# Moving the table of gates by token behind the large SBUF pools

## The chip, the cores and the metric

The kernel runs on one core of one Trainium2 chip. The metric is the device time of one execution in microseconds (us); the time of a kernel is the median of its runs. Below, a profile of one execution is used beside it.

## The reference

Attention with a sliding window of 128 keys and 4 sink keys, for 4 batches, 8 heads, 768 tokens and a head width of 64; its output, 3072 tokens by 512, goes through a mixture of 4 experts, all of which are computed for each token and added with weights from a given table:

```python
keep = is_sink | in_window              # rel = query - key in [0, 128), or key < 4
scores = np.where(keep, scale * q @ k.T, -1e9)
a = softmax(scores);  x = a @ v         # x as [B*S, H*D] = [3072, 512]
p = domain_probs / (domain_probs.sum(-1, keepdims=True) + 1e-09)
for e in range(4):                      # w1[e] is 512 x 1024, w2[e] is 1024 x 512
    out += p[:, e:e + 1] * (np.maximum(x @ w1[e], 0.0) @ w2[e])
```

## The kernel before

Everything works on tiles of 128 partitions in bf16, with sums in PSUM in float32. Batches go one after another, each in three groups of 256 tokens, and for each group each of the four experts is a unit of work.

**Stages.** Queries, keys and values of a batch are loaded by POOL's queue with a cast from float32 to bf16 (`qkn`, line 267, and `vx`, line 331); the weights `w1` and `w2` likewise (lines 344 and 354). The first 256 tokens of q and k come in float32 by SP's and ACT's queues (line 292, tiles `qraw` and `kraw`) and are cast on DVE and ACT. Batch 0 is turned on TensorE (line 616); the later batches are turned by DMA transposes on SP's queue: `qkT` from `qkn` (line 276), `xT` from `onat` (line 806). Scores (line 719) go through ACT's exponential (line 747) into `aT`; `aT` is multiplied with the values `vx` (line 789) and, for the sink keys, `sinkA` with `vsd` (line 782).

**Experts.** The first product of an expert is made directly for early units (line 1134), later with seven products of half blocks (line 1224); for late units with the operands exchanged (line 1336), so that the result lies token by token. There it is multiplied by the gate of each token, one number for each partition, from `own_gates` (lines 1357 and 1361), and a DMA transpose turns it into `H` (line 1317). The other units multiply by rows of gates that were spread over all partitions (`gates`, lines 491, 1158 and 1257). The second product is line 1597 for the first two groups and line 1511 for the others.

**Order.** The kernel is planned in Python while it is written out: it keeps an estimated clock for each engine and for both kinds of DMA queue, and at each step emits the piece of work that is ready first, by fixed priorities. The order on every engine is thus fixed when the program is built. While TensorE would be idle in the first 20 us, idle products on a tile of zeros (`lent`, line 595) are put in.

**Where tiles lie in SBUF.** The pools are laid end to end, each tile rounded up to 32 bytes in every partition, in this order: `consts`, `wpool` (weights and their combinations), `attn_sb`, `moe_sb`, `odd`. The first free byte is 16512. In `consts` come first six tiles `vx` of 1056 bytes each (8 heads, 66 bf16 numbers for each head, of which 65 are used), then `own_gates` (18 x 4 float32, 288 bytes, line 327), then `gates0`, `gates1` (2048 bytes each), `ident`, `masks`, `ksd`. From the end of `own_gates` on, up to the pool `odd`, every tile has a size that is a multiple of 256 bytes.

Before, `own_gates` begins at byte 22848 and `gates0` at 23136, which is 96 past a multiple of 256, and so does each tile of the pools `wpool`, `attn_sb` and `moe_sb` after it. In the pool `odd` lie small tiles: `held`, `vsf` (the values of the sinks), `scale_t`, `sel2`, `half`, `own_sum`, six `R`, `vsd` and `rs`.

Small tiles that the change names: `scale_t` (line 511) holds the gates of the first two groups, loaded by SP at line 1691, made ready in `gates()` with `rs` (line 961) and read at lines 1607 and 1610. `sel2` (line 520) and `half` (line 579) are constants for the sinks; `held` (line 498) is the target of two small copies on POOL (line 1726), which make it wait.

Of the kernel before, what the change touches and what calls it, by code (L numbers as in the profile page):

```python
# [11 lines left out]
FP32 = mybir.dt.float32  # L12
BF16 = mybir.dt.bfloat16
# [3 lines left out]
def kernel(  # L17
# [17 lines left out]
    E, Dm, F = moe_w1.shape  # L35
    Ntok, Dout = out.shape

    P = 128
# [7 lines left out]
    NHP = H // 2  # L46
# [52 lines left out]
    NEARLY = 2  # L99
# [39 lines left out]
    def dve(cols, *deps, rate=0.96, fixed=157):  # L139
        at = max([t["dve"], *deps])  # L140
        t["dve"] = at + fixed - 77 + cols / rate
        return at + fixed + 60 + cols / rate

    def pool(cols, *deps, fixed=190):
        at = max([t["pool"], *deps])
        t["pool"] = at + fixed + cols * 1.8
        return t["pool"] + 35
# [96 lines left out]
    consts = ctx.enter_context(tc.tile_pool(name="consts", bufs=1))  # L244
# [3 lines left out]
    odd = ctx.enter_context(tc.tile_pool(name="odd", bufs=1))  # L248
# [75 lines left out]

    vx = [consts.tile([P, H, DP], BF16, name=f"vx{tb}") for tb in range(NQB)]
    OWNED = 2 * NG * (B - OWN)
    own_gates = consts.tile([P, OWNED, E], FP32, name="own_gates")

    def load_v(b, ts):
        for tb in ts:  # L330
            nc.gpsimd.dma_start(  # L331
                out=vx[tb][:, :, 0:D],
                in_=v[b, :, tb * P:(tb + 1) * P, :].rearrange("h p d -> p h d"),
            )
            lands(("v", b, tb), H * P, D, values_at[b - 1, min(NG - 1, (tb + 1) // 2)] if b else 0.0)
# [159 lines left out]
        gate_at[pair, e] = sp(mix.finished[mix.gated[len(gate_sb) - 1 - NGATE]] if len(gate_sb) > NGATE else 0.0, takes=300) + GATE_LANDS  # L495


    held = odd.tile([P, 2], BF16, name="held")
    nc.vector.memset(identf, 1.0)
    lent = wpool.tile([P, 12 * P], BF16, name="lent", tag=f"wf_{E - 2}")  # L500
    zeros = lent[:, 0:4 * P]
# [4 lines left out]
    for h in range(H):  # L506
# [1 line left out]
        nc.sync.dma_start(  # L508
            out=vsf[r:r + NSINK, :, 0:D], in_=v[:, h, 0:NSINK, :].rearrange("b j d -> j b d"),
        )  # L510
    scale_t = odd.tile([P, 2 * NEARLY, E], FP32, name="scale_t")
    ident = consts.tile([P, P], BF16, name="ident")
    load_v(0, (0,))
    for sgn in (1, -1):
# [2 lines left out]
            base=0, pattern=[[sgn, P]], channel_multiplier=-sgn,  # L517
        )
        pool(0, fixed=320)
    sel2 = odd.tile([P, NHP, 2], FP32, name="sel2")  # L520
    load_v(0, (1,))
    t["sw"] += 500
    for tb in (2, 3):
# [52 lines left out]
    t["dve"] += 240.0  # L576

    vsd = {}
    half = odd.tile([P, 2], BF16, name="half")
    ksd = [consts.tile([P, NHP, 32], BF16, name=f"ksd{i}") for i in range(2)]  # L580

    nc.vector.memset(half, 0.0)
# [375 lines left out]


    def gates():  # L960
        rs = odd.tile([P, 2 * NEARLY], FP32, name="rs")
        nc.vector.reduce_sum(out=rs, in_=scale_t, axis=AX.X)
        nc.vector.tensor_scalar_add(out=rs, in0=rs, scalar1=1e-9)
        nc.vector.reciprocal(out=rs, in_=rs)
        nc.vector.tensor_mul(scale_t, scale_t, rs[:, :, None].to_broadcast([P, 2 * NEARLY, E]))
        dve(200)
# [8 lines left out]
    class Mixture:  # L975
# [608 lines left out]
        def emit_second(self):  # L1584
            ready = self.second_ready()
            g, s, e = self.second.pop(0)
            if g not in out_sb:
                out_sb[g] = mo.tile([P, 2, Dout], FP32, name="osbw", tag=f"wide{g}", bufs=1)
                if g == 0:
                    gates()  # L1590
# [232 lines left out]
```

## Time and profile before

| | |
|---|---|
| median of 3 runs | 353.85 us (353.6 to 354.17) |
| profiled execution, device time | 354.31 us |
| its span, first to last instruction | 352.6 us |
| TensorE matmuls (PE) busy | 345.2 us, 98% |
| weight loads (PEld), DVE, ACT, POOL busy | 76%, 80%, 59%, 20% |
| DMA packets | 161800, of them 145508 under 512 bytes; 45.62 MB |
| granted TensorE clock | 1.000 |

The profile is that of one execution. "Busy" is the time from the start of an engine's instructions to their end; matmuls overlap one another, so a matmul's own duration (273 ns for 256 columns) is longer than the time from one to the next. The chain of waits follows the work back from the last instruction, at each step to what released it. A window names the busy time of each engine in a stretch of the span.

### The profile page before, as it was taken

How to read it: one execution, taken by the hardware profiler on the slowest of the kernel's cores; microseconds unless marked ns; L12 is line 12 of the kernel's file. 1: busy time of each engine (PE TensorE's matmuls, PEld its weight loads, DVE VectorE, ACT ScalarE, POOL GpSimd, SP SyncE). 2: the span in 40 equal slices, each digit the busy share in tenths (PEclk: the TensorE clock that was granted, in tenths of full speed). 3: DMA queues.
4: the chain of work that ended last, by engine and by line, in shares of the span. 5: the costliest groups of instructions: out<-in, count | busy, mean ns of one | idle time of the engine just before them, and what ended most of it. 6: DMA issues, size and time to landing. Idle time of an engine off the chain costs nothing.

```text
span 352.6 us, 9328 instructions
## 1 busy us (share of the span) xinstructions
PE 345.2 (98%) x3699; PEld 266.7 (76%) x3722; DVE 282.9 (80%) x672; ACT 207.5 (59%) x481; POOL 72.0 (20%) x89
## 2 busy tenths in 40 slices
PE   8999999999999999999999999999999999999996
PEld 4685869756798998899999886756856666666785
DVE  5785889988999999899799899488769594785740
ACT  4864813446645734856544559489589666757411
POOL 8946104340242351400144000000000000000000
PEclk9999999999999999999999999999999999999999
DMA  9999999999995999950799905339338838455431
GB/s 171 172 191 192 220 217 173 182 159 145 181 133 55 170 175 146 134 100 26 80 175 149 138 32 98 84 71 156 75 91 168 131 60 164 78 105 135 89 92 61
DMA packets 161800, 45.62 MB, mean 129 GB/s; under 512 B 145508, under 2 KB 157764, under 8 KB 161756
## 3 DMA queue, kind: packets, MB, share of 16 engines
q0 software_dynamic: 79104, 17.31, 55.2%
q1 hardware_dynamic: 81596, 27.19, 42.1%
q8 instruction: 29, 0.48, 0.6%
q10 hardware_dynamic: 1056, 0.52, 0.6%
q14 instruction: 15, 0.12, 0.1%
HBM read 38.40 MB, written 6.34 MB: 127 GB/s over the span
## 4 chain that ended last, share of the span: by engine, by line
PE 89%; DMA 3%; POOL 2%; ACT 2%; DVE 1%; issue 1%; POOLq 0%; ACTq 0%
PE acc L1511 34%; PE cps L1224 18%; PE cps L1336 14%; PE hps L1134 8%; PE acc L1597 8%; PE sps L719 3%; PE od L789 3%; DMA w<-in_moe_w_dram 2%; POOL qkn L267 1%; POOL vx L331 1%; PE od L782 1%; DMA H<-rest 1%; DVE cps L1384 1%; PE sinks L680 0%; DVE gates L1361 0%
## 5 line engine op out<-in xcount | busy, mean ns | idle before, releaser
L1511 PEld LDWEIGHTS <-H 128*128 128x128 bf16 x708 | 66.2, 98 | 18.4 <-issue 1.6
L1511 PE MATMUL acc<-w,H 128*128 128x256 bf16 x420 | 57.3, 273 | 0.3 <-ACT acc L1550 0.2
L747 ACT ACTIVATE aT<-sps 128x512 bf16<-128x512 f32 (+1 forms) x96 | 47.4, 577 | 12.5 <-PE sps L719 12.4
L1224 PEld LDWEIGHTS <-w 128*128 128x128 bf16 x640 | 39.3, 98 | 1.7 <-issue 0.6
L1511 PEld LDWEIGHTS <-S 128*128 128x128 bf16 x320 | 30.8, 98 | 8.5
L1257 DVE SCALAR_TENSOR_TENSOR H<-cps,gates 128x512 bf16<-128x512 f32 x54 | 36.3, 684 | 0.6 <-PE cps L1224 0.4
L834 ACT ACTIVATE onat<-od,R 128x64 bf16<-128x64 f32 x120 | 27.4, 332 | 14.4 <-DVE R L816 11.9
L1134 PE MATMUL hps<-xT,w 128*128 128x256 bf16 x256 | 32.2, 273 | 0.7 <-DMA w<-in_moe_w_dram 0.7
L331 POOL DMA_DIRECT2D vx<-in_v_dram x24 | 21.3, 892 | 55.6 <-PE od L789 43.3
L1354 ACT ACTIVATE cps<-cps 128x512 f32<-128x512 f32 x41 | 23.8, 585 | 14.9 <-PE cps L1336 14.0
L1511 PE MATMUL acc<-wf,H 128*128 128x256 bf16 (+1 forms) x224 | 30.9, 271 | 0.1
L1224 PEld LDWEIGHTS <-vf 128*128 128x128 bf16 x480 | 29.2, 98 | 0.9 <-issue 0.5
L1597 PE MATMUL acc<-w,H 128*128 128x512 bf16 x121 | 29.2, 379 | 0.4
L1134 PEld LDWEIGHTS <-w 128*128 128x128 bf16 x256 | 24.0, 98 | 5.3 <-DMA w<-in_moe_w_dram 0.9
L739 DVE TENSOR_TENSOR aT<-aT,masks 128x1024 bf16<-128x1024 bf16 (+1 forms) x36 | 22.8, 644 | 4.4 <-ACT aT L747 4.2
L1572 ACT COPY osb<-acc 128x256 f32<-128x256 f32 x32 | 12.1, 379 | 22.8 <-PE acc L1511 22.7
L1224 PE MATMUL cps<-T,w 128*128 128x128 bf16 x320 | 24.3, 219 | 0.0
L1224 PE MATMUL cps<-T,vf 128*128 128x128 bf16 x320 | 23.8, 219 | 0.0
L1224 PE MATMUL cps<-xT,w 128*128 128x128 bf16 x320 | 23.7, 219 | 0.0
L267 POOL DMA_DIRECT2D qkn<-in_q_dram x22 | 19.7, 896 | 16.3 <-DMA qkT<-qkn 8.5
L1336 PE MATMUL cps<-w,T 128*128 128x512 bf16 x75 | 22.7, 379 | 0.1
L1336 PE MATMUL cps<-vf,T 128*128 128x512 bf16 x77 | 22.6, 379 | 0.1
(144 smaller groups left out, 673.1 us busy)
## 6 DMA issues: line engine op xcount, KB each, us to landing
w<-in_moe_w_dram POOLq DMA_DIRECT2D x6, 1024.0 KB, 18.6
out_dram<-osb SPq DMA_DIRECT2D x16, 256.0 KB
vx<-in_v_dram POOLq DMA_DIRECT2D x24, 128.0 KB, 6.6
qkn<-in_q_dram POOLq DMA_DIRECT2D x22, 128.0 KB, 6.9
qkn<-in_k_dram POOLq DMA_DIRECT2D x22, 128.0 KB, 7.2
gates<-gate_rows SPq DMA_DIRECT2D x20, 128.0 KB
w<-in_moe_w_dram POOLq DMA_DIRECT2D x4, 256.0 KB, 8.0
w<-in_moe_w_dram POOLq DMA_DIRECT2D x2, 512.0 KB, 11.4
```

Source lines behind the costliest of these rows:

```text
L267: nc.gpsimd.dma_start(out=nat[b, tb][:, i], in_=(q, k)[i][b, :, tb * P:(tb + 1) * P, :].rearrange("h p d -> p h d"),)
L331: nc.gpsimd.dma_start(out=vx[tb][:, :, 0:D], in_=v[b, :, tb * P:(tb + 1) * P, :].rearrange("h p d -> p h d"),)
L739: nc.vector.tensor_mul(x, x, m[:, None, :].to_broadcast([P, 2 if g == 0 else 4, w if g == 0 else 2 * P]))
L747: nc.scalar.activation(out=a[:, ph], in_=sps[ph][:, 0:w], func=AF.Exp, scale=scale)
L834: nc.scalar.mul(o[:, qi, hp, ph * D:(ph + 1) * D], od[:, qi, ph, 0:D], R[:, qi, ph])
L1134: nc.tensor.matmul(h[:, i].rearrange("p (q n) -> p q n", q=2), lhsT=w1_sb[e][:, db, fb * P:(fb + 1) * P], rhs=xT[b, g][:, :, db], start=(i ...
L1224: nc.tensor.matmul(y[:, f], lhsT=A[:, d, f * P:(f + 1) * P], rhs=T[:, d], start=(m in ("P1", "P5") and f == 0 and d == 0), stop=(d == 1), ...
L1257: nc.vector.scalar_tensor_tensor(out=dst, in0=src, scalar=0.0, in1=gate, op0=ALU.max, op1=ALU.mult)
L1336: nc.tensor.matmul(y.rearrange("p f n -> p (f n)"), lhsT=T[:, d], rhs=A[:, d], start=(m in ("P1", "P5") and d == 0), stop=(d == 1), skip_g ...
L1354: nc.scalar.activation(out=src, in_=src, func=AF.Relu)
L1511: nc.tensor.matmul(y, lhsT=self.operand(b, g, e, m)[:, f], rhs=forms[e][m][:, f, cs], start=(k == 0 and f == 0 and m in (("P1", "P5", "P2" ...
L1597: nc.tensor.matmul(op, lhsT=H[:, fb // QF, fb % QF, s], rhs=w2_sb[e][:, fb, :], start=(fb == 0), stop=(fb == NFB - 1),)
```

## The change

`own_gates` leaves the pool `consts` and becomes a tile of `odd`, the last pool. In its place stand five small tiles that were in `odd`. No instruction is added or taken away.

```diff
-    own_gates = consts.tile([P, OWNED, E], FP32, name="own_gates")
+    own_gates = odd.tile([P, OWNED, E], FP32, name="own_gates")
+    scale_t = consts.tile([P, 2 * NEARLY, E], FP32, name="scale_t")
+    sel2 = consts.tile([P, NHP, 2], FP32, name="sel2")
+    held = consts.tile([P, 2], BF16, name="held")
+    half = consts.tile([P, 2], BF16, name="half")
+    rs = consts.tile([P, 2 * NEARLY], FP32, name="rs")
...
-    held = odd.tile([P, 2], BF16, name="held")
...
-    scale_t = odd.tile([P, 2 * NEARLY, E], FP32, name="scale_t")
...
-    sel2 = odd.tile([P, NHP, 2], FP32, name="sel2")
...
-    half = odd.tile([P, 2], BF16, name="half")
...
 def gates():
-        rs = odd.tile([P, 2 * NEARLY], FP32, name="rs")
```

With each tile rounded up to 32 bytes the five take 64 + 32 + 32 + 32 + 32 = 192 bytes where `own_gates` took 288. So `gates0` begins at 23040 = 90 x 256, and all tiles behind it, up to the pool `odd`, lie 96 bytes lower than before. `vx` stays where it was. In `odd`, `own_gates` now begins at a multiple of 256, `vsf` goes from 128 to 32 past such a multiple, and `vsd` from 64 to 96 past it.

## The prediction

> **What bounds the kernel now.** I read the page first, for the engine that the time hangs on and for the chain of waits that ended last.
>
> ```profile
> span 352.6 us, 9328 instructions
> PE 345.2 (98%) x3699; PEld 266.7 (76%) x3722; DVE 282.9 (80%) x672; ACT 207.5 (59%) x481; POOL 72.0 (20%) x89
> ...
> PE 89%; DMA 3%; POOL 2%; ACT 2%; DVE 1%; issue 1%; POOLq 0%; ACTq 0%
> ```
>
> TensorE (PE) is busy for 98% of the span and has 89% of the chain. A change can help in two ways only: matmuls follow each other at shorter intervals, or PE waits less. So I next took the windows, to see how much waiting there is and where.
>
> ```profile
> 0.00:18.25 18.25, 15.59 (x151) 9.09 (x152) 12.12 (x55) 11.95 (x28) 16.58 (x24) 1.00 1.68 173
> 18.25:40.00 21.75, 21.59 (x228) 15.50 (x230) 15.50 (x47) 14.04 (x28) 10.08 (x13) 1.00 1.56 197
> 40.00:90.00 50.00, 49.67 (x499) 36.02 (x504) 45.39 (x90) 22.62 (x54) 13.15 (x15) 1.00 1.63 178
> 90.00:210.00 120.00, 119.95 (x1736) 108.87 (x1735) 112.70 (x261) 66.47 (x188) 32.16 (x38) 1.00 1.07 122
> 210.00:352.60 142.60, 138.43 (x1092) 97.24 (x1104) 97.18 (x224) 92.38 (x188) 0.00 (x0) 1.00 0.51 103
> ```
>
> The columns are the stretch, its length, then busy time of PE, weight loads, DVE, ACT and POOL. PE's idle time is length less busy: 2.66, 0.16, 0.33, 0.05 and 4.17 us. Of the first and the last, the two rows of the timeline below take a part: nothing runs on PE before 1.40, and its last matmul ends at 349.04 + 0.39 = 349.43, which leaves 352.60 - 349.43 = 3.17 us for the last copy and store.
>
> ```profile
> 1.40 4.88 PE L595 MATMUL acc<-lent 128*128 128x512 bf16 x13 [1.40 <-DVE lent L502]
> ```
>
> ```profile
> 349.04 0.39 PE L1511 MATMUL rest<-qkn,qkT 128*128 128x128 bf16 x4
> ```
>
> So between its first and last matmul PE is idle for 1.26 us until 18.25, for 0.54 us until 210, and for 1.00 us after that: **2.8 us in all**. The chain of waits says what is late at the start:
>
> ```profile
> 3.96 3.72 POOL qkn L267 x4
> 7.68 1.75 POOL vx L331 x2
> 9.43 0.70 POOL w L344
> 10.13 8.05 DMA w<-in_moe_w_dram
> 18.17 0.05 issue
> 18.22 1.05 PE hps L1134 x8
> ```
>
> POOL issues loads until 10.13, then the first weights have to land, and at 18.22 the first product that needs them goes on. From there on the chain is nearly all PE.
>
> **The change, part by part.** It moves tiles and nothing else. In the two built programs each of the five engines has the same instructions in the same order with the same waits, so no step, DMA or queue is passed by another. Two groups of addresses change. (1) All large tiles behind the gate table, from `gates` to `H` and the output tiles, move down by 96 bytes, from 96 past a multiple of 256 to the multiple. Their places against each other stay. (2) A handful of small tiles change pools. So the question is only whether an access to SBUF costs something else at another start address. I go through those who access it.
>
> *TensorE.* The cost of an interval is read from runs of equal matmuls in the chain of waits.
>
> ```profile
> 32.85 1.73 PE acc L1597 x8
> ...
> 55.70 7.15 PE cps L1224 x128
> ...
> 102.03 3.06 PE acc L1511 x28
> ```
>
> 512 columns take 1.73/8 = 216 ns, 128 columns 7.15/128 = 55.9 ns, and 256 columns 3.06/28 = 109.3 ns. The first two give (216.3 - 55.9)/384 = 0.418 ns for each column and 2.4 ns for each matmul beside its columns; for 256 columns that gives 109.3, as seen. Those 2.4 ns are all that a start address could take part in: 3699 x 2.4 = 8.9 us, the lower bound. All these operands lie 96 past a multiple of 256. Two kinds of matmul in the trace read at other starts: line 782 reads `vsd`, at 64 past a multiple of 256 and then every 260 bytes, and line 789 reads `vx`, every 132 bytes.
>
> ```profile
> 19.27 0.06 PE od L782
> 19.32 0.12 PE od L789 x4
> 19.45 0.06 PE od L782
> 19.50 0.12 PE od L789 x4
> ```
>
> By the law above 130 columns take 130 x 0.418 + 2.4 = 57 ns and 65 columns 30 ns; the rows have 0.06 us and 0.12/4 = 30 ns. Starts that differ in every way carry the same 2.4 ns. I take **0** for PE. Weight loads (266.7 us) run beside the matmuls and stay covered; were one late, it would show in these intervals.
>
> *DVE and ACT.* They have 1% and 2% of the chain, so a change of theirs counts only through PE's 2.8 us. For DVE two rows compare starts:
>
> ```profile
> L1277 DVE TENSOR_TENSOR cps<-H,cps 128x512 f32<-128x512 f32 x20 | 13.9, 693 | 2.6 <-PE cps L1224 2.0 <-ACT aT L747 0.5
> L658 DVE TENSOR_TENSOR vsd<-vsf,sel 128x520 bf16<-128x520 f32 x3 | 2.1, 695 | 0.0
> ```
>
> With `H` at 96 past a multiple of 256, 512 numbers take 693 ns; with `vsf` at 128 and `vsd` at 64, 520 take 695 ns. I take 0, for ACT too, for which I have no such pair; the chain's 2% stands for its weight.
>
> *Loads into SBUF.* Here `vx` and `qkn` can be set beside each other: equal size (128 KB), same queue, both cast from float32. `qkn` has its rows of 128 bytes at 96 and 224 past multiples of 256; `vx` every 132 bytes. The page's rows are medians, the other two the extremes (first `vx`, then `qkn`):
>
> ```profile
> vx<-in_v_dram POOLq DMA_DIRECT2D x24, 128.0 KB, 6.6
> qkn<-in_q_dram POOLq DMA_DIRECT2D x22, 128.0 KB, 6.9
> qkn<-in_k_dram POOLq DMA_DIRECT2D x22, 128.0 KB, 7.2
> ```
>
> ```profile
> DMA to landing us min/median/max: 3.2/6.6/21.2
> ```
>
> ```profile
> DMA to landing us min/median/max: 3.6/7.1/29.0
> ```
>
> The raggedest target lands no later than the more regular one, neither in the median nor at best. I take **0** for loads, the nearer end. The other end is that the start is freed of all its idle time, -1.26 us. Above 0, I see no reason why a row that begins at a multiple of 256 should land later than one that begins 96 past it.
>
> *Transposes and stores, which read SBUF by DMA.* All their sources lie 96 past a multiple of 256, so the trace has no other start to set beside them. What they could give is bounded by who waits. One transpose is long on the chain, and PE's idle time behind it is in brackets:
>
> ```profile
> 236.38 3.21 DMA H<-rest
> ```
>
> ```profile
> 244.92 1.25 PE L1511 MATMUL acc<-w,H 128*128 128x256 bf16 x10 [0.20 <-ACT acc L1550]
> ```
>
> PE idles 0.20 us there. So -0.20 us and 0 are the ends, and -0.10 is my value, in the middle, since no row is nearer to either. The last stores are in the 3.17 us behind the last matmul; they are small and I take 0.
>
> *Small tiles.* `own_gates` is read as one number for each partition, `scale_t` likewise, `sel2` and `half` a few times at the start. Each is an access of a few bytes on an engine with slack; 0. `vsd` goes from 64 to 96 past a multiple: priced in the second rival.
>
> **Sum:** 0 + 0 + 0 - 0.10 + 0 = -0.1 us. The profiled execution took 354.31 us, 1.71 more than its span, and 0.46 more than the median of the runs, 353.85; the sum taken from the median gives **353.75 us**.
>
> **The rivals.**
>
> *The start is freed (faster).* The loads before the first product land earlier when their rows begin at multiples of 256: `qraw`, `kraw`, `qkn`, `w1`. For it: the chain's 8.05 us on the first weights, a DMA wait that everything behind 18.22 hangs on. Against it: the landings of `vx`. It gives at most the 1.26 us of idle time up to 18.25 and the 0.20 us of the transpose: 353.85 - 1.46 = 352.4 us; PE's fixed order and its idle products set that limit.
>
> [...]
>
> *PE loses on the values (slower).* `vx` stays while `aT` moves by 96 bytes, and `vsd` moves by 32 against `sinkA`. If reading weights and moving rows at once hinders when their addresses agree in some low bits, lines 789 and 782 would take longer. The trace has the spread of line 789:
>
> ```profile
> L789 PE MATMUL od<-vx,aT x352: 190/193/204, 9.0 to 267.8; 128*128 128x65 bf16 x176
> ```
>
> From the median 193 to the longest 204 ns it is 11 ns; all 352 at the longest cost 3.9 us, 357.7 us in all, and it decides from 2 ns each (0.7 us). Against it: the six `vx` tiles have six different starts, and medians and extremes lie close.
>
> *PE gains (faster).* If the fixed 2.4 ns were the price of the 96 bytes, all of it would give 345 us, 1 ns of it 350.2. The rows of lines 782 and 789 speak against it.
>
> *The change does not do what it says.* The move is the sum of sizes, 192 for 288 bytes, so it does; only `vx` keeps its odd starts. This has no time of its own.
>
> **How the numbers follow.** A measurement of this kernel can tell about 0.2%, or 0.7 us, from no change. The forecast has 0.66: its own range is 353.1 to 354.5, the median and 0.7 either way. The freed start has 0.16, and half of its size or more is over the bound. PE's gain has 0.05, the loss on the values 0.13, as the one way I can name for the time to rise. That makes faster 0.21, same 0.66, slower 0.13. The range takes in the forecast's own and the freed start down to 352.4: 352.4 to 354.5, which holds 0.82.
>
> **What would show it right or wrong.** In the profile after: 512, 256 and 128 columns again at 216, 109 and 56 ns (PE: 0); lines 782 and 789 at 0.06 and 0.12 us for one and four (second rival); the first product behind the weights again near 18.2 us, with a DMA wait near 8 us ahead of it (if it comes a whole us earlier, the first rival is right); medians of the `qkn` landings near 7 us, and of `vx` near 6.6; the transposes' issues and the wait on `H` at 236. A time below 353.1 with unchanged intervals would mean that SBUF reads or writes by DMA do depend on the start; one above 354.5 that something pays for the alignment, and I would look at lines 789 and 782 first.

## The result and the profile after

The changed kernel takes **353.02 us** (median of 9 runs, 352.37 to 353.24), the kernel before 353.73 us in runs on the same chip (9 runs, 353.56 to 354.17). The ratio is 0.9974, with a 95% interval from 0.9964 to 0.9984: faster by 0.71 us, or 0.2%, just past the 0.7 us that the prediction drew as the bound between "same" and "faster". The nine times after lie in two groups, 352.37, 352.38 and 352.54, and six from 352.88 to 353.24; those of before do not. The profiled execution after took 353.11 us. That of before, 354.31 us, was 0.46 us above its median, so the two profiles differ by 1.20 us and the medians by 0.71. Two executions further down lie far outside and are left out of the ratios: one of 509.94 us in `all_but_mo` and one of 915.66 us in `small_only`.

The page of after, with the share of SP's queue, the chain by engine and some landings:

```profile
span 351.4 us, 9351 instructions
PE 346.1 (99%) x3722; PEld 266.7 (76%) x3722; DVE 282.8 (80%) x672; ACT 207.2 (59%) x481; POOL 71.6 (20%) x89
...
q1 hardware_dynamic: 81596, 27.19, 39.4%
...
PE 95%; DVE 2%; ACT 1%; issue 0%; DVEq 0%
...
vx<-in_v_dram POOLq DMA_DIRECT2D x24, 128.0 KB, 5.7
qkn<-in_q_dram POOLq DMA_DIRECT2D x22, 128.0 KB, 8.0
...
w<-in_moe_w_dram POOLq DMA_DIRECT2D x4, 256.0 KB, 6.9
```

The same queue and the same weights on the page of before:

```profile
q1 hardware_dynamic: 81596, 27.19, 42.1%
...
w<-in_moe_w_dram POOLq DMA_DIRECT2D x4, 256.0 KB, 8.0
```

Every engine is as busy as before. What moved are DMAs: SP's queue takes 39.4% of the DMA engines' time for the same 81596 packets and 27.19 MB, where it took 42.1%, and the pieces of 256 KB of the weights land after 6.9 us instead of 8.0. The chain of waits, which had 3% of DMA, has none. Part of the last two readings belongs to the one execution of before that was profiled: in the profile of `small_only`, a kernel described below whose large tiles lie at 96 as in before, the chain has no DMA either, and the weights land after 7.5 us. (3722 matmuls stand where there were 3699: the program has the same number, but 23 records are missing in the trace of before.)

Where on the clock the time went is read from three places. **The start**, in the timeline of PE of after:

```profile
15.94 1.04 PE L1134 MATMUL hps<-xT,w 128*128 128x256 bf16 x8
16.91 0.39 PE L720 MATMUL sps<-qkT 64*128 64x128 bf16 x6
17.36 1.03 PE L1134 MATMUL hps<-xT,w 128*128 128x256 bf16 x8
```

The product that waited for weights until 18.22 now begins at 17.36, with no wait in brackets. That wait too was the profiled execution's: in `small_only` the same product begins at 17.39 without it, and in none of the eleven other profiles of the table further down does it wait for weights. The chain of waits of after, with the runs of equal matmuls:

```profile
20.81 0.06 PE od L783
20.87 0.12 PE od L790 x4
...
22.73 3.33 PE hps L1134 x29
...
32.13 1.73 PE acc L1597 x8
...
54.98 7.15 PE cps L1224 x128
...
101.22 3.06 PE acc L1511 x28
```

and the run of 29 products in that of before:

```profile
23.45 3.33 PE hps L1134 x29
```

The durations are those of before to the last digit. The offset between the kernels is 23.45 - 22.73 = 0.72 us at the first long run and 102.03 - 101.22 = 0.81 at the last: it arises before 23 us, and in the next 78 us only 0.09 comes on top. Some 0.4 of the 0.72 is probably that execution's own, since its time lay 0.46 above the median.

**Late**, the offset grows again. The timeline of SP's queue, whose transposes (line 1317) turn results into `H`, first before, then after; the columns are start, length, what is issued and how often:

```profile
233.94 5.06 SPq L1317 DMA_TRANSPOSE H<-rest  x3
...
241.50 2.81 SPq L1317 DMA_TRANSPOSE H<-gates  x2
...
278.07 13.39 SPq L1317 DMA_TRANSPOSE qkT<-rest  x5
```

```profile
233.13 5.04 SPq L1317 DMA_TRANSPOSE H<-rest  x3
...
240.20 2.81 SPq L1317 DMA_TRANSPOSE H<-gates  x2
...
276.84 13.39 SPq L1317 DMA_TRANSPOSE qkT<-rest  x5
```

The offset is 0.81 us at the first row, 1.30 at the second and 1.23 at the third. From the first to the third row pass 44.13 us before and 43.71 after: **0.42 us** less. This stretch is used as a measure below.

**Inside a transpose**, the windows while the first of the five at 278 run almost alone, two of them back to back before and a single one after; the last two columns are the busy share of the DMA engines (above 1 where packets overlap) and GB/s, before and then after:

```profile
279.30:282.00 2.70, 2.70 (x22) 1.85 (x20) 0.74 (x2) 1.45 (x4) 0.00 (x0) 1.00 1.00 192
```

```profile
278.05:279.05 1.00, 1.00 (x10) 0.71 (x8) 0.00 (x0) 0.65 (x2) 0.00 (x0) 1.00 1.15 259
```

A transpose of 256 KB reads 1024 rows of 256 bytes (1024 packets of 256 bytes in the traces of before and after). At 192 GB/s that is 262144/192 = 1.37 us, at 259 GB/s 1.01 us. By the middle rows above SP issues two within 2.81 us, 1.4 us each: at 1.37 us for each transfer, with stores in between, they can queue up behind each other, at 1.01 us there is room.

### The profile page after: what moved, and what is told of

The parts are those of the page before. It is cut to its first block, busy times and chain, and to the rows that moved or that the text cites. A ratio compares the mean times of both kernels' runs of the same rounds, so it can differ in the third digit from the quotient of the medians.

```text
span 351.4 us, 9351 instructions
## 1 busy us (share of the span) xinstructions
PE 346.1 (99%) x3722; PEld 266.7 (76%) x3722; DVE 282.8 (80%) x672; ACT 207.2 (59%) x481; POOL 71.6 (20%) x89
## 3 DMA queue, kind: packets, MB, share of 16 engines
q1 hardware_dynamic: 81596, 27.19, 39.4%
## 4 chain that ended last, share of the span: by engine, by line
PE 95%; DVE 2%; ACT 1%; issue 0%; DVEq 0%
PE acc L1511 35%; PE cps L1224 18%; PE cps L1336 17%; PE acc L1597 8%; PE hps L1134 7%; PE sps L720 3%; PE od L790 3%; PE acc L596 2%; PE od L783 1%; DVE aT L758 1%; PE tx L854 1%; DVE onat L820 0%; PE tr L617 0%; PE sinks L681 0%; ACT aT L748 0%; DVE T L1190 0%
## 5 line engine op out<-in xcount | busy, mean ns | idle before, releaser
L1336 PE MATMUL cps<-w,T 128*128 128x512 bf16 x80 | 23.8, 379 | 0.0
L1336 PE MATMUL cps<-w,xT 128*128 128x512 bf16 x80 | 23.5, 379 | 0.0
```

The costliest lines, as they stand in the source:

```text
L1336: nc.tensor.matmul(y.rearrange("p f n -> p (f n)"), lhsT=T[:, d], rhs=A[:, d], start=(m in ("P1", "P5") and d == 0), stop=(d == 1), skip_g ...
```

## The experiments

**Theories.** The first: a DMA row in SBUF that crosses a multiple of 256 bytes costs more, in the loads of the start and in the transposes, and this is the whole gain. Its rivals: the five small tiles and `own_gates` did it by their new places; the engines gained; or the start differs from execution to execution and the change has nothing to do with it. Within the first theory three things are open: which of the two ends of a transfer counts, whether the distance from the multiple counts, and which tiles matter.

In the edits `consts` is the pool that lies first, `attn_sb` holds `qkn`, `rest`, `onat` and others, and `moe_sb` holds `qraw`, `kraw`, `H` and the output tiles. A pad moves all that lies behind it.

### The addresses alone, the small tiles alone

`pad_only` is the kernel before with 160 unused bytes, so that the large tiles begin at multiples of 256 and the small ones stay in `odd`:

```diff
     own_gates = consts.tile([P, OWNED, E], FP32, name="own_gates")
+    consts.tile([P, 40], FP32, name="pad")
```

> The kernel before with 160 unused bytes behind the gate table: the large tiles begin at multiples of 256, the small tiles stay in their pools. Theory (DMA rows that begin at the multiple land earlier, so the first weights and some transposes come sooner): as the changed kernel, about 0.7 us under before (353.0 us), first product behind the weights about 0.7 us before the 18.2 us of the kernel before, share of the SP queue's packets near 39.4%. Rival (the small tiles' new places do it): within 0.2 us of before, first product near 18.2 us, share near 42%.

`small_only` is the changed kernel with 96 unused bytes, so that the small tiles are moved and the large ones lie at 96 as before:

```diff
     rs = consts.tile([P, 2 * NEARLY], FP32, name="rs")
+    consts.tile([P, 24], FP32, name="pad")
```

> The changed kernel with 96 unused bytes behind the five small tiles: the small tiles have moved, the large tiles begin 96 past a multiple of 256 as before. Theory: as the kernel before, 353.7 us, first product near 18.2 us, share of the SP queue's packets near 42%. Rival (the small tiles' new places do it): as the changed kernel, 353.0 us, share near 39.4%.

Measured: `pad_only` 352.45 us, ratio to before 0.9965 (0.9951 to 0.9978); `small_only` 353.98 us, ratio 1.0001 (0.9992 to 1.001). The stretch on SP's queue is 276.18 - 232.47 = 43.71 us in the first and 277.37 - 233.26 = 44.11 us in the second. The window of transposes in `small_only`:

```profile
278.60:281.30 2.70, 2.70 (x22) 1.84 (x20) 0.75 (x2) 1.45 (x4) 0.00 (x0) 1.00 1.00 191
```

191 GB/s are before's 192. The gain belongs to the addresses of the large tiles; the small tiles do nothing that can be measured. That `pad_only` lies below after is looked at further down.

### Does the distance from the multiple count?

`at64` and `at128` are the changed kernel with 64 or 128 unused bytes ahead of the large tiles:

```diff
     rs = consts.tile([P, 2 * NEARLY], FP32, name="rs")
+    consts.tile([P, 16], FP32, name="pad")
```

> The changed kernel with 64 unused bytes there: the large tiles begin 64 past a multiple of 256. If the boundary that counts is one of 64 bytes: as the changed kernel, 353.0 us, SP queue share near 39.4%. If it is 256 with the bytes ahead of a row paid for: a 256-byte row covers 320 bytes instead of 352 at 96 past and 256 at 0, so about two thirds of the way from 0 to 96: 353.5 us, share near 41%. If only a start at 128 or 256 helps: as before, 353.7 us.

```diff
     rs = consts.tile([P, 2 * NEARLY], FP32, name="rs")
+    consts.tile([P, 32], FP32, name="pad")
```

> The changed kernel with 128 unused bytes there: the large tiles begin 128 past a multiple of 256. If the boundary that counts is one of 64 or 128 bytes: as the changed kernel, 353.0 us, SP queue share near 39.4%. If it is 256 with the bytes ahead of a row paid for: a 256-byte row covers 384 bytes, more than at 96 past, so above the kernel before, about 353.9 us, and a share above 42%.

Measured: `at64` 353.85 us, 0.9998 (0.9989 to 1.0006); `at128` 353.55 us, 0.9993 (0.9985 to 1.0002). The windows of transposes, first `at64`, then `at128`:

```profile
278.45:281.15 2.70, 2.70 (x21) 1.85 (x20) 0.76 (x2) 1.45 (x4) 0.00 (x0) 1.00 1.00 191
```

```profile
278.70:281.40 2.70, 2.70 (x22) 1.85 (x20) 0.74 (x2) 1.45 (x4) 0.00 (x0) 1.00 1.00 192
```

At 64, 96 and 128 past the multiple the transposes move 191, 191 and 192 GB/s, and the stretch on SP's queue is 44.11, 44.11 and 44.10 us. In these runs it counts whether a row crosses a multiple (191 to 192 GB/s) or not (259 in after), not where; why a crossing row is slower, no run shows. If the bytes ahead of a row were paid for, the 320, 352 and 384 bytes that the expectations count at 64, 96 and 128 would have the three differ by up to a fifth; 191, 191 and 192 GB/s do not.

At 128 a row of 128 bytes ends at a multiple and crosses none, while one of 256 bytes crosses. In the first 18.25 us the DMA engines of `at128` are indeed less loaded (1.55, as in after; 1.71 in `at64`). Its time is 0.30 us below that of `at64`, in the direction of a gain at the start alone; its interval holds 1. Neither expectation, 353.0 or 353.9 us, came: the transposes are as slow as at 96, and the engines at the start are as little loaded as in after.

### Which end of the transposes, and which tiles?

`all_but_mo` is the changed kernel with a pad at the start of `moe_sb`: `H`, the target of the transposes, lies at 96, and their sources in `attn_sb` and `consts` at multiples of 256. It ran a second time as `all_but_mo_2`, from which its profile is taken.

```diff
+        mo.tile([P, 24], FP32, name="pad", tag="pad", bufs=1)
         raw = {name: mo.tile([P, 2, 4, 2 * D], FP32, name=f"{name}raw", ...
```

> The changed kernel with 96 unused bytes ahead of the pool moe_sb: weights, their combinations, qkn, qkT, aT, onat and xT begin at multiples of 256, while qraw, kraw, H and the output tiles begin 96 past one. The transposes into H then read a row at the multiple and write at 96 past it. Theory (a DMA row that crosses a multiple of 256 costs more where it is read): transposes as short as in the changed kernel, the 0.4 us between 237 and 266 us gained, about 353.1 to 353.3 us. Rival (the write side pays): those transposes as long as before, nothing gained there, about 353.6 us.

> Once more the changed kernel with qraw, kraw, H and the output tiles 96 past a multiple of 256, for a profile at full clock. Read-side theory: transposes from rest and gates short though H lies 96 past a multiple, 353.1 us as in the first run of it. Rival (the write side pays too): those transposes between 1.06 and 1.38 us.

`only_mo` is the reverse, the kernel before with `moe_sb` alone at multiples of 256:

```diff
+        mo.tile([P, 40], FP32, name="pad", tag="pad", bufs=1)
         raw = {name: mo.tile([P, 2, 4, 2 * D], FP32, name=f"{name}raw", ...
```

> The kernel before with 160 unused bytes ahead of the pool moe_sb: only qraw, kraw, H and the output tiles begin at multiples of 256. The transposes into H read at 96 past a multiple and write at the multiple. Read-side theory: transposes as long as before, no gain between 237 and 266 us, about 353.7 us. Write-side rival: the 0.4 us there gained, about 353.4 us. If the first rows (qraw, kraw) alone free the start: another 0.3 us or so earlier at 25 us.

Measured: `all_but_mo` 353.12 us, 0.9977 (0.9967 to 0.9987), and 353.15 us, 0.998 (0.9971 to 0.9989), the second time; `only_mo` 353.32 us, 0.9985 (0.9976 to 0.9994). The windows of transposes, first `all_but_mo_2`, then `only_mo`:

```profile
278.15:279.10 0.95, 0.95 (x9) 0.66 (x8) 0.00 (x0) 0.61 (x2) 0.00 (x0) 1.00 1.19 268
```

```profile
278.30:280.95 2.65, 2.65 (x20) 1.81 (x19) 0.70 (x2) 1.40 (x4) 0.00 (x0) 1.00 1.03 195
```

The transposes in these windows read `rest` and write `qkT`, both in `attn_sb`: with both ends at the multiple they move 268 GB/s over these 0.95 us (268 in after too, from 278.08 to 279.03), with both at 96 195 GB/s. The two ends come apart on SP's queue, where the transposes write `H`. With the source at the multiple and the target at 96 the stretch is 276.91 - 233.20 = 43.71 us, as in after, and its first part, from the first row to the second, 7.06 us (7.07 in after); with the target at the multiple and the source at 96 they are 277.06 - 232.87 = 44.19 us and 7.57 us (7.56 in before). In a transpose it is the **reading** end that pays. `only_mo` gains all the same, so its 0.52 us under the 353.84 that before took in the same session can't come from the transposes: `qraw`, `kraw`, `H` and the output tiles are all that it aligns, and by the rows further down the gain stands at the start, where `qraw` and `kraw` are loaded.

`only_attn` is the kernel before with `attn_sb` alone at multiples of 256, `only_w` the changed kernel with everything but `consts` and the weights at 96:

```diff
+        mo.tile([P, 24], FP32, name="pad", tag="pad", bufs=1)
...
+    sb.tile([P, 40], FP32, name="pads", tag="pads", bufs=1)
     first = {name: sb.tile([P, 2, H, D], BF16, name="qkn", ...
```

> Only the pool attn_sb begins at a multiple of 256 (qkn, qkT, aT, onat, xT and the halves of H named rest); gates, weights, qraw, kraw and H stay 96 past one. Read-side theory: transposes from rest, qkn and onat as short as in the changed kernel (packets of one within 1.06 us instead of 1.38), those from gates long; most of the 0.4 us between 237 and 266 us gained, and part of the start: about 353.3 us. Rival (sources and targets must both begin at the multiple): transposes into H long, about 353.6 us.

```diff
+    sb.tile([P, 24], FP32, name="pads", tag="pads", bufs=1)
     first = {name: sb.tile([P, 2, H, D], BF16, name="qkn", ...
```

> The changed kernel with 96 unused bytes ahead of the pool attn_sb: only gates, constants, weights and their combinations begin at multiples of 256. Theory (the start hangs on when the first weights have landed, and qkn and the raw rows are ahead of them): most of the start's gain missing, at 25 us within 0.2 us of the kernel before, 0.1 us or less gained later (only the halves of gates serve as sources of transposes): about 353.6 us. Rival (the weights' own rows make the start): 0.3 us or more earlier at 25 us, about 353.4 us.

Measured: `only_attn` 353.07 us, 0.998 (0.9971 to 0.9989), stretch 43.71 us; `only_w` 353.74 us, 0.9996 (0.9987 to 1.0005), stretch 44.02 us. So `attn_sb` by itself brings as much as the change does by its median, and the weights by themselves, whose slow landing had ended the chain's long wait in the profile of before, bring nothing that can be measured.

### Why after lies in two groups, and a faster kernel

The profiles of after and `pad_only` differ by 0.69 us, and all of it stands at the start. TensorE begins with 13 idle products, 9 of 512 columns and 4 of 256; a row of the timeline names one shape only. Their rows, and the 29 products further on, in after (its 22.73 is shown above) and `pad_only`:

```profile
1.41 4.88 PE L596 MATMUL acc<-lent 128*128 128x512 bf16 x13 [1.41 <-DVE lent L506]
```

```profile
1.41 3.96 PE L596 MATMUL acc<-lent 128*128 128x512 bf16 x13 [1.41 <-DVE lent L503]
```

```profile
22.06 3.33 PE hps L1135 x29
```

The same 13 products take 4.88 us in one execution and 3.96 in the other; at the pace of later they would take 9 x 216 + 4 x 109 ns = 2.4 us. The starts of the single products in the traces show two paces: at first those of 512 columns follow each other after 427 ns, from some moment on after 216. That moment is 4.33 us in `pad_only` and 6.80 us in after, where the idle products are over by then and the first transposes on TensorE are slow too (one each 107 ns, where 56 is the pace of later). So the 29 products come 0.67 us earlier. 427 and 216 ns are about two to one, and over the profiles the moment lies between 4.33 and 7.44 us; what sets it, no run shows. The granted clock in the windows is 1.00 throughout and doesn't show it.

So the start has two conditions, PE at full pace and the loads landed. To tell them apart two idle products are left out, in the changed kernel (`seven_idle`) and in the kernel before (`before_seven`); the planner's clock counts them as before, so all else stays in its order:

```diff
-        for _ in range(n):
-            nc.tensor.matmul(x[:, 0:cols], lhsT=zeros[:, 0:P], ...
+        for i in range(n):
+            if n < 9 or i < 7:
+                nc.tensor.matmul(x[:, 0:cols], lhsT=zeros[:, 0:P], ...
             pe(cols)
```

> The changed kernel without the last two of the nine 512-column idle products at the start (the plan still counts nine). They compute nothing that is used. In the profile of the kernel with 160 unused bytes the 13 idle products took 3.96 us, in the others 4.88, and its whole course was 0.66 us earlier. Theory (with the loads earlier the end of the idle products holds the start up): two fewer, 0.85 us at the slow pace, let the first transposes begin near 5.5 us instead of 6.07 in every execution: about 352.4 us. Rival (the slow pace lasts until enough products have run, so fewer of them only make the following work slower; or the loads hold the start up): no gain, 353.0 us or more.

> The kernel before (large tiles 96 past a multiple of 256) without the last two of the nine 512-column idle products, as in the run that took 352.44 us with the tiles at the multiples. Theory (the start needs both: the idle products out of the way, and the loads landed): the early start is lost again before 25 us to the loads, which land as late as in the kernel before; 353.6 to 353.9 us, so the alignment is worth about 1.3 us once the idle products are cut. Rival (the idle products alone hold up the start): 353.85 - 0.6 = 353.2 us or less.

Measured: `seven_idle` **352.44 us** (352.42 to 352.51, 5 runs), ratio 0.9958 (0.9945 to 0.997); `before_seven` 353.85 us, 0.9999 (0.999 to 1.0008). The idle products, what follows them and the 29 products, from the timeline and the chain of `seven_idle`:

```profile
1.40 3.63 PE L597 MATMUL acc<-lent 128*128 128x512 bf16 x11 [1.40 <-DVE lent L506]
5.50 0.62 PE L618 MATMUL tr<-ident,qkn 128*128 128x128 bf16 x8 [0.47 <-DVE qkn L300]
5.96 0.27 PE L597 MATMUL acc<-lent 128*128 128x256 bf16 x1
...
6.49 0.34 PE L721 MATMUL sps<-qkT 64*128 64x128 bf16 x4
```

```profile
22.08 3.33 PE hps L1135 x29
```

and of `before_seven`:

```profile
1.40 4.02 PE L596 MATMUL acc<-lent 128*128 128x512 bf16 x11 [1.40 <-DVE lent L502]
5.49 1.05 PE L617 MATMUL tr<-ident,qkn 128*128 128x128 bf16 x8
6.33 0.42 PE L596 MATMUL acc<-lent 128*128 128x256 bf16 x1
...
7.31 0.34 PE L720 MATMUL sps<-qkT 64*128 64x128 bf16 x4
```

```profile
9.40 0.28 PE L790 MATMUL od<-vx,aT 128*128 128x65 bf16 x4 [0.19 <-DMA vx<-in_v_dram]
```

```profile
23.10 3.33 PE hps L1135 x29
```

The times came as expected, but the two profiles can't show why. Both turn to real work at 5.50 and 5.49 us, and then differ in pace: one product of 256 columns takes 0.27 us in `seven_idle` and still 0.42 in `before_seven`, whose first scores begin 0.82 us later, mostly for that reason. So the 23.10 - 22.08 = 1.02 us between their 29 products can't be put down to the loads alone.

Two profiles at one pace are those of `only_w` and `pad_only`, where the full pace comes at 4.35 and 4.33 us. At the start they differ in the rows of `qraw`, `kraw` and `qkn`, at 96 in the first and at multiples in the second, and in the small tiles, which do nothing. The 29 products begin at 23.12 and 22.06 us: with the rows at multiples of 256 the early start lasts, without, **1.06 us** of it are lost. In `only_w` TensorE soon waits for a load:

```profile
9.46 0.28 PE L791 MATMUL od<-vx,aT 128*128 128x65 bf16 x4 [0.15 <-DMA vx<-in_v_dram]
```

Over all profiles, with the start of the first product at full pace ("full pace from") and the medians from issue to landing of the first two loads of `vx` and the first four of `qkn`:

| kernel | tiles at multiples of 256 | full pace from, us | `vx` lands after, us | `qkn` lands after, us | 29 products begin | SP stretch, us | median, us |
|---|---|---|---|---|---|---|---|
| `seven_idle` | all | 4.54 | 6.0 | 5.3 | 22.08 | 43.71 | 352.44 |
| `pad_only` | all | 4.33 | 5.9 | 5.2 | 22.06 | 43.71 | 352.45 |
| after | all | 6.80 | 5.9 | 5.3 | 22.73 | 43.71 | 353.02 |
| `only_attn` | `attn_sb` | 5.56 | 6.4 | 5.5 | 22.61 | 43.71 | 353.07 |
| `all_but_mo_2` | all but `moe_sb` | 6.25 | 6.7 | 5.8 | 22.80 | 43.71 | 353.15 |
| `only_mo` | `moe_sb` | 5.11 | 6.0 | 5.8 | 22.27 | 44.19 | 353.32 |
| `at128` | none, but rows of 128 bytes cross none | 7.44 | 6.6 | 5.7 | 22.96 | 44.10 | 353.55 |
| `only_w` | `consts`, weights | 4.35 | 6.9 | 6.5 | 23.12 | 44.02 | 353.74 |
| before | none | 6.47 | 6.5 | 6.2 | 23.45 | 44.13 | 353.73 |
| `at64` | none | 5.77 | 6.5 | 6.6 | 22.68 | 44.11 | 353.85 |
| `before_seven` | none | 6.9 to 7.3 | 6.8 | 6.6 | 23.10 | 44.19 | 353.85 |
| `small_only` | none | 6.37 | 6.6 | 6.4 | 22.76 | 44.11 | 353.98 |

**Which loads.** No run moves `vx`, but its first two loads land after 5.9 to 6.0 us where `qraw` and `kraw`, loaded at the same time, begin at multiples (the pool `moe_sb`), and after 6.4 to 6.9 elsewhere. The `qkn` land after 5.2 to 5.3 us with both `qraw`, `kraw` and their own rows right, after 5.5 to 5.8 with one of the two, `at128` among them, and after 6.2 to 6.6 with neither. So both kinds of rows pay where they are written, and each gives about half a microsecond of landing.

**What it brings.** In the seven upper rows the 29 products begin the earlier, the earlier the full pace comes, but for one pair: 22.06 and 22.08 us at 4.33 and 4.54, 22.27 at 5.11, 22.61 at 5.56, 22.80 at 6.25, 22.73 at 6.80, 22.96 at 7.44. In the lower five no such order is seen; `only_w`, with the earliest pace of these, is among the latest. The alignment takes the loads out of the way, so that TensorE's own pace decides. What is left of it when that pace comes late can't be read from single profiles: after's 22.73 stands beside 22.76 in `small_only` and beside 23.45 in before, whose execution had its own wait for weights.

The rest of each execution is the same to some tenths. From the first product of line 1134, which begins between 15.27 and 16.33 us, to the end of the profiled execution's time pass 337.14 to 337.17 us in the five kernels whose `attn_sb` lies at multiples, 337.56 to 337.81 in six of the others, and 338.11 in before. So the gain has two parts: 0.4 to 0.7 us behind that product, most of which the stretch of the transposes shows, and what the start gives in each execution.

The two groups of after's times fit this: its profiled execution (353.11 us) has the full pace from 6.80 us, that of `pad_only` (352.42 us) from 4.33. The other executions have no trace, so that all of them divide by the pace is not shown. Times under 352.6 us came only with all large tiles at multiples, `qraw` and `kraw` too: in 3 of 9 runs of after, 4 of 5 of `pad_only` and all 5 of `seven_idle`, but in none of the 30 of `only_attn` and `all_but_mo`. Whether `seven_idle` owes its five to the two products left out is open too: in its profile the full pace came at 4.54 us anyway, and TensorE then stood for 0.47 us until a cast of `qkn` was done. At the 7 in 14 of after and `pad_only`, five in a row come about once in 32 by luck.

## Why the prediction was right, and where its sizes were off

The forecast of 353.75 us was 0.73 us above the 353.02 that came. The time fell from the median as forecast, by seven times the 0.10 us of the sum. The forecast's own range ended at 353.1, and the measurement lies below that; only the wider range, let down to 352.4 for the rival of the freed start, holds it. So it was right by its hedge and not by its sum. Its sign "a time below 353.1 with unchanged intervals" is what came, and its meaning, that DMA does depend on the start of a row, is what the runs show.

*TensorE, 0:* right. 512, 256 and 128 columns take 216, 109 and 55.9 ns as before, and lines 783 and 790 (782 and 789 of before) again 0.06 and 0.12 us. By that the rival "PE gains" and the slower rival "PE loses on the values" both fell.

*DVE and ACT, 0, and the small tiles, 0:* right; DVE is busy for 282.9 and 282.8 us, ACT for 207.5 and 207.2, and `small_only` at 1.0001 carries the small tiles at new places. (`vsd` lies at 192 past a multiple there and at 96 in after; line 783 takes 0.06 us in after.)

*Loads, "I take 0 for loads, the nearer end":* this step failed. Aligned loads are worth about 0.3 us of the 0.71 between the medians (what the 0.42 of the transposes leaves), and 1.06 us where TensorE is ready early (`only_w` beside `pad_only`). The comparison on which the 0 rested, `qkn` with `vx`, had no power. `qkn` rows of 128 bytes at 96 and 224 cross a multiple of 256 every second time; `vx` rows, every 132 bytes, cross one in 3 or 4 of 8 cases. Two tiles with the same share of crossing rows can't tell what a crossing costs. Nor do landing medians over the whole run: with the change `qkn` went from 6.9 to 8.0 us and `vx`, which did not move, from 6.6 to 5.7. Landings of equal pieces lie between 3.2 and 21.2 us over the run (`vx` of before), so that, by an estimate, the medians hold above all what else was under way. The first four `qkn` alone show it, 6.2 us before and 5.3 after, and so does the busy share of the DMA engines in the first 18.25 us, 1.68 and 1.55. Of the loads that the prediction named, `qraw`, `kraw` and `qkn` gained and `w1` by itself did not (`only_w`).

*Transposes, -0.10 with -0.20 as the far end:* the sign was right, the size was not, and neither was the end: 0.42 us came. The bound took PE's idle time in the row at 244.92 for all that there was. The transposes form a queue: the offset grew by 0.49 us between 234 and 241.5 on SP, ahead of that row, since each one's end and the next one's begin add up. And a stop shorter than the overlap of matmuls can leave no idle time behind it: a matmul of 256 columns is recorded with 273 ns and the next follows after 109, so up to 0.16 us of waiting can lie inside records that look busy. No run separates the two. Here PE's idle time, 0.20 us, was no upper bound on what the waits cost.

*"2.8 us in all" of idle time:* part of it was not there. Windows from 40 to 90 and from 90 to 210 of after:

```profile
40.00:90.00 50.00, 50.00 (x510) 35.88 (x508) 45.48 (x88) 22.12 (x53) 13.13 (x15) 1.00 1.63 184
90.00:210.00 120.00, 120.00 (x1737) 108.95 (x1735) 112.65 (x261) 67.25 (x191) 31.88 (x38) 1.00 1.06 119
```

Here PE is never idle, where before showed 49.67 and 119.95. Before lacks 23 matmul records, and a gap between records counts as idle. Up to 18.25 the idle time was real and shrank from 2.66 to 1.89 us, but 0.66 of it was the wait for weights that no other profile has:

```profile
0.00:18.25 18.25, 16.36 (x159) 10.03 (x160) 12.36 (x55) 12.23 (x28) 16.98 (x25) 1.00 1.55 178
```

*"The start is freed", 352.4 us at 0.16:* this rival had the mechanism for `qraw`, `kraw` and `qkn`. That its figure is nearly that of `pad_only` and `seven_idle` (352.45 and 352.44) is luck, since its sum has other parts: it gave the start all its 1.26 us and the transposes 0.20. Its argument, the chain's 8.05 us on the first weights, and its sign, the first product behind them a whole us earlier, both hung on the one execution of before; that product came at 17.36 us in after and at 17.39 in `small_only`, which gains nothing. In the kernel as changed the start is freed in some executions only, which the prediction had no term for.

What stays open: what sets the moment of the full pace in an execution; whether leaving out two idle products makes the early start sure; and how large the gain of the start is when the full pace comes late, since the medians' 0.3 us mixes executions of either kind.

## What to carry to other kernels

Where DMA transposes read SBUF in rows of 256 bytes, as here, try rows that begin at multiples of 256 (259 GB/s in after where before had 192): a pad of 160 bytes ahead of the large pools was enough (`pad_only`, 352.45 us), and it was the source of a transpose that had to be aligned, not its target (43.71 and 44.19 us in `all_but_mo_2` and `only_mo`). Rows that a load writes gained too, here those of 512 bytes that begin at a multiple and those of 128 that cross none (the first `qkn` land after 5.2 to 5.3 us with both, after 6.2 to 6.6 with neither). Before two tiles are set beside each other to price an address, count for each how many of its rows are in the state that is to be priced. Before a wait in one profile is made the reason for a change, look whether it stands in a second profile. When a kernel's times lie in groups, look for a second condition at the start that varies between executions; in these profiles the start came early only where both were met.

## What the runs showed of the hardware

A transpose from SBUF to SBUF with rows of 256 bytes moved 257 to 259 GB/s over 1.00 us where its rows begin at multiples of 256 (`only_attn`, `pad_only`, after) and 191 to 195 GB/s at 64, 96 and 128 past them. The start of the target alone made no difference: the stretch of the transposes took 43.71 us with `H` at 96 past and its sources at the multiple, 44.19 with `H` at the multiple and its sources at 96. Loads into SBUF paid as well: the first four of `qkn`, in rows of 128 bytes, landed after 5.5 to 5.8 us where their rows cross no multiple and `qraw` and `kraw` lie at 96 or 128, after 6.2 to 6.6 where both cross. The first matmuls of each profiled execution ran at half the pace, 427 ns for 512 columns and later 216, until a moment that lies between 4.33 and 7.44 us in these profiles. TensorE showed no dependence on whether operands begin at 0 or 96 past a multiple of 256 (216, 109 and 55.9 ns at both), nor did VectorE (681 ns for `H` from `cps` and `gates` in `pad_only` and in `small_only`).
